# One planned order for all engines: a list scheduler inside a fused attention and maxout kernel

## The chip, the cores and the metric

The kernel runs on one NeuronCore of one Trainium2 chip. The metric is device time in microseconds (us) of that core. A run is one execution; a profiled run also leaves a trace, whose span (first to last instruction) is about 2 us shorter than the run's time. Runs are called slow here when they are over 1.5% above the fastest run of the same kernel.

Engine names: PE is TensorE, DVE is VectorE, ACT is ScalarE, POOL is GpSimd, SP is the engine that issues DMAs here.

## The reference, cut to what matters

```python
def _attn_ref(q, k, v, is_retrieval, n_sink, window):    # q, k, v: (4, 8, 768, 64)
    scores = scale * np.matmul(q, k.transpose(0, 1, 3, 2))
    ...   # retrieval heads: causal; the others: causal and (in a window of 64 or one of 4 sinks)
    scores = np.where(mask[None, :, :, :], scores, -1000000000.0)
    a = np.exp(scores - np.max(scores, axis=-1, keepdims=True))
    a = a / (np.sum(a, axis=-1, keepdims=True) + 1e-09)
    return np.matmul(a, v)

def reference(...):
    x = attn_out.transpose(0, 2, 1, 3).reshape(B * S, H * D)    # 3072 x 512
    return np.maximum(x @ w1, x @ w2) @ w_out                   # d_ff = 1024
```

## The kernel before

The maxout is rewritten as max(x·w1, x·w2) = relu(x·(w1−w2)) + x·w2, so the dense part needs `wd` = w1−w2, and the merged matrix `wm` = w2·w_out, which the kernel builds itself. Attention goes by pairs of heads, 16 pairs in all, four to a batch. A pair needs: loads of q, k, v; casts to bf16 on POOL; PE transposes of q and k, copied out of PSUM; scores in six steps (`S`), exponentials on ACT, masks on DVE; value products (`A`); a normalisation on DVE; a transpose of x (`X`). The dense work of batch b (up matmuls `U`, ReLU, down matmuls `D`) fills PE in the pairs of batch b+1; that of the last batch stands alone at the end.

Only PE is held to the order of the program. The other queues are ordered by the framework's own scheduler. PE's order is written by hand, and a quota decides how much dense work goes into each gap:

```python
    def prep_wd():
        for c in range(KC):
            nc.vector.tensor_sub(out=wd_bf[:, c, :], in0=wts["w1"][:, c, :], in1=w2_bf[:, c, :])
    ...
        # transpose_pair: q's copy always on DVE, k's always on ACT, both strided
        o = t.rearrange("q (m p r) -> q m r p", p=128, r=2)
        i = psb[:, 0:S].rearrange("q (m r p) -> q m r p", p=128, r=2)
        if which == 0:
            nc.vector.tensor_copy(out=o, in_=i)
        else:
            nc.scalar.copy(out=o, in_=i)
    ...
                nc.vector.tensor_relu(out=gts[g][:, f, :], in_=ps[:, 0:GT])     # ReLU always on DVE
    ...
                    nc.scalar.copy(out=ot, in_=ps)                              # output always on ACT
    ...
    with tc.manual_schedule(engines={mybir.EngineType.PE}):
        ...
        for i, cur in enumerate(pairs):
            ...
            if i == 3:
                prep_wo()
                prep_wd()
                fill += [(FC * 512, lambda c=c: w_merge(c)) for c in range(KC)]
            left = 12 - 3 * (i % HP) if b > 0 else 3
            quota = sum(c for c, _ in fill) / left / 3
            first = prev is not None and hp == 0      # first pair of a batch
            qk(*cur, 0)
            if not first:
                spend(quota)
            if prev:
                av(*prev, 4)
                ...
                av(*prev, 5)
            ...
            if first:
                xtr(*prev)
            qk(*cur, 1)
            spend(quota)
            ...
```

The softmax here doesn't subtract the row's maximum and nothing guards it: scores larger than these inputs give would overflow.

## Time and profile before

| | before |
|---|---|
| time, median of 2 runs | 247.19 us (246.89 to 247.49) |
| span of the profiled run, mean granted PE clock | 244.7 us, 0.963 |
| PE, DVE, ACT, POOL busy | 83%, 58%, 52%, 22% |
| first biased exponential of the fifth pair (end of the batch-0 stage) | 61.5 us |
| last x transpose (end of attention) | 213.0 us |

The biased exponential of a pair (`far0` in the code) occurs once per head and marks how far the pair has come. It follows the pair's first scores by 1.4 to 2.1 us, and it is the marker.

From the page of the kernel before: engine, busy us, share of the span, instructions; then busy tenths, PE's granted clock in tenths and the DMA rate in 40 equal slices of 6.1 us.

```profile
...
PE 203.1 (83%) x1888; PEld 114.9 (47%) x1888; DVE 141.0 (58%) x307; ACT 127.2 (52%) x233; POOL 53.8 (22%) x76
...
PE   0587878268599898995998999959989999799994
...
ACT  2387666205626584666657755763747548301001
...
PEclk9999999959689999999999999997999999999999
...
GB/s 142 276 386 227 312 407 291 321 309 234 181 12 11 228 202 145 67 215 161 80 64 110 43 110 0 85 46 0 4 32 57 43 3 43 88 0 43 86 46 86
...
```

PE looks busy from the twelfth slice on, but not before: in the eighth slice (43 to 49 us) it is busy for 20 to 29%. The granted clock drops in slices after that one. PE's busy time also hides waits: the Trainium skill ("Perfetto Trace Analysis", section on per-engine timelines) says that the end of a matmul is estimated by the profiler and not observed. This trace agrees in that eight value matmuls at 108.37 us show 0.41 us, while the next group starts 0.24 us after they did. So the text prices PE's work by starts.

The chain of waits of the kernel before, 38 to 62 us (start, us, what): what the end of batch 0 hung on.

```profile
...
42.66 0.31 DVE wd_bf L157
42.97 0.97 issue
43.95 1.84 DVE wd_bf L157
45.78 0.47 DVE x L284
...
46.74 3.52 DVE wd_bf L157 x2
50.26 0.48 DVE x L284
...
52.27 3.41 PE wmp L169 x8
...
```

DVE did the four wd subtractions between a reciprocal and the multiplication that belongs to it, and between masks. PE had to wait for that normalisation to free its bank, and the next scores stand behind it in PE's fixed order. On ACT the timeline shows one wait of 11.6 us (last bracket: idle before, and who ended it):

```profile
...
56.15 0.87 ACT L231 ACTIVATE at<-sc 128x384 bf16<-128x384 f32 x2 [11.60 <-PE sc L222]
...
```

The timeline at a batch boundary (first pair of the third batch):

```profile
...
111.42 0.61 PE L222 MATMUL sc<-qt,kt 64*128 64x256 bf16 x6
...
111.96 0.48 PE L245 MATMUL po<-vb,at 128*128 128x65 bf16 x10
...
112.58 1.09 DVE L235 TENSOR_TENSOR at<-at,msk 128x512 bf16<-128x512 bf16 x1 [2.87 <-ACT at L231]
...
114.68 0.56 DVE L284 TENSOR_TENSOR x<-po,rez 128x384 bf16<-128x384 f32 x1
...
115.29 0.51 PE L293 MATMUL xtp<-ident,x 128*128 128x128 bf16 x6 [2.85 <-DVE x L284]
...
```

PE ends the value products at about 112.4 us and has nothing queued until the last normalisation on DVE (`x`, from 114.68) is done: 2.85 us idle. DVE is late because it took masks first, and masks wait for ACT.

### The profile page before, as it was taken

Reading aid. Unit: us, or ns where it says so; the run is one execution under the profiler, and the core shown is the slowest. Engines: PE = TensorE matmul, PEld = TensorE weight load, DVE = VectorE, ACT = ScalarE, POOL = GpSimd, SP = SyncE. Lnnn points to the kernel's source line nnn. Section 1 sums busy time; section 2 is a strip of 40 time slices with the busy share of each in tenths; the row PEclk is TensorE's granted clock in tenths of the full one; section 3 lists DMA queues with packets and bytes.
Section 4 is the critical chain, followed back from the end, with each engine's and each line's share of the span. In section 5 each row is a group of like instructions: output and inputs, shape, how many; then the busy total and the mean of one; then the engine's idle time right before and its main releaser. Section 6 shows DMA issues by size and latency. Waiting matters only on the chain.

```text
span 244.7 us, 4799 instructions
## 1 busy us (share of the span) xinstructions
PE 203.1 (83%) x1888; PEld 114.9 (47%) x1888; DVE 141.0 (58%) x307; ACT 127.2 (52%) x233; POOL 53.8 (22%) x76
## 2 busy tenths in 40 slices
PE   0587878268599898995998999959989999799994
PEld 0254654134364545552545555525545555454541
DVE  6966595964666448454864384646653854570510
ACT  2387666205626584666657755763747548301001
POOL 0738381910312121212121211221110100000000
PEclk9999999959689999999999999997999999999999
DMA  5998999998600865285224140210001101201212
GB/s 142 276 386 227 312 407 291 321 309 234 181 12 11 228 202 145 67 215 161 80 64 110 43 110 0 85 46 0 4 32 57 43 3 43 88 0 43 86 46 86
DMA packets 55686, 31.77 MB, mean 130 GB/s; under 512 B 25968, under 2 KB 50544, under 8 KB 55664
## 3 DMA queue, kind: packets, MB, share of 16 engines
q1 hardware_dynamic: 55520, 31.46, 42.9%
q8 instruction: 15, 0.25, 0.4%
q14 instruction: 7, 0.06, 0.1%
q10 hardware_dynamic: 144, 0.01, 0.0%
HBM read 25.17 MB, written 6.29 MB: 129 GB/s over the span
## 4 chain that ended last, share of the span: by engine, by line
PE 62%; DVE 17%; ACT 12%; issue 3%; DMA 2%; POOL 2%; SPq 0%; ACTq 0%; POOLq 0%
PE y L324 26%; PE h L307 12%; PE sc L222 10%; ACT at L231 7%; DVE at L235 6%; PE po L245 5%; PE tp L194 4%; ACT kt L201 3%; PE wmp L169 3%; DVE gt L310 3%; DVE x L284 2%; DMA kn<-in_k_dram 2%; DVE wd_bf L157 2%; PE xtp L293 2%; ACT ot L327 2%
## 5 line engine op out<-in xcount | busy, mean ns | idle before, releaser
L231 ACT ACTIVATE at<-sc 128x512 bf16<-128x512 f32 (+1 forms) x96 | 48.8, 561 | 57.5 <-PE sc L222 57.5
L235 DVE TENSOR_TENSOR at<-at,msk 128x512 bf16<-128x512 bf16 (+1 forms) x96 | 42.7, 451 | 50.5 <-ACT at L231 48.9
L307 PE MATMUL h<-xt,wd_bf 128*128 128x384 bf16 x256 | 51.8, 335 | 2.5 <-DVE gt L310 1.7
L324 PE MATMUL y<-wo_bf,gt 128*128 128x512 bf16 x192 | 48.4, 380 | 0.0
L310 DVE TENSOR_SCALAR gt<-h 128x384 bf16<-128x384 f32 x64 | 35.0, 554 | 19.2 <-PE h L307 18.2
L245 PEld LDWEIGHTS <-at 128*128 128x128 bf16 x672 | 34.3, 104 | 21.8 <-DVE x L284 7.2
L245 PE MATMUL po<-vb,at 128*128 128x65 bf16 x672 | 39.3, 203 | 6.2 <-DVE x L284 6.2
L222 PE MATMUL sc<-qt,kt 64*128 64x256 bf16 (+3 forms) x320 | 32.4, 309 | 5.0 <-ACT kt L201 4.4
L231 ACT ACTIVATE at<-sc,bias_j 128x512 bf16<-128x512 f32 (+1 forms) x64 | 34.0, 593 | 0.0
L307 PEld LDWEIGHTS <-wd_bf 128*128 128x128 bf16 x256 | 23.4, 99 | 21.0 <-issue 10.1
L327 ACT COPY ot<-y 128x512 f32<-128x512 f32 x24 | 14.1, 589 | 35.0 <-PE y L324 34.8
L324 PE MATMUL y<-wm_bf,xt 128*128 128x512 bf16 x96 | 24.6, 379 | 3.5 <-ACT ot L327 2.6
L201 ACT COPY kt<-tp 128x768 bf16<-128x768 bf16 x16 | 16.3, 1020 | 20.8 <-PE tp L194 20.8
L185 POOL CAST vb<-vn 128x768 bf16<-128x768 f32 x16 | 14.7, 918 | 46.4 <-PE po L245 31.0
L182 POOL CAST kb<-kn 128x768 bf16<-128x768 f32 x16 | 15.6, 977 | 41.0 <-PE tp L194 40.3
L324 PEld LDWEIGHTS <-gt 128*128 128x128 bf16 x192 | 16.4, 98 | 17.2 <-issue 3.0
L222 PEld LDWEIGHTS <-kt 64*128 64x128 bf16 x320 | 13.0, 100 | 22.7 <-issue 10.6
L182 POOL CAST qb<-qn 128x768 bf16<-128x768 f32 x16 | 13.9, 870 | 35.2 <-issue 27.0
L231 ACT ACTIVATE at<-sc,bias_94 128x512 bf16<-128x512 f32 x32 | 20.3, 697 | 0.0
L199 DVE COPY qt<-tp 128x768 bf16<-128x768 bf16 x16 | 16.3, 1018 | 3.6 <-PE tp L194 3.2
L194 PE MATMUL tp<-ident,qb 128*128 128x128 bf16 x96 | 9.8, 250 | 8.9 <-DVE bias_94 L128 7.2
L284 DVE TENSOR_TENSOR x<-po,rez 128x384 bf16<-128x384 f32 x32 | 16.8, 552 | 0.1
(41 smaller groups left out, 116.2 us busy)
## 6 DMA issues: line engine op xcount, KB each, us to landing
qn<-in_q_dram SPq DMA_DIRECT2D x16, 384.0 KB, 5.3
kn<-in_k_dram SPq DMA_DIRECT2D x16, 384.0 KB, 4.5
vn<-in_v_dram SPq DMA_DIRECT2D x16, 384.0 KB, 4.8
out_dram<-ot SPq DMA_DIRECT2D x24, 256.0 KB, 2.0
w_151<-in_moe_w_dram SPq DMA_DIRECT2D x2, 1024.0 KB, 9.3
wo<-in_moe_w_out_dram SPq DMA_DIRECT2D x2, 1024.0 KB, 7.6
w_169<-in_moe_w_dram SPq DMA_DIRECT2D x2, 1024.0 KB, 10.9
ir_raw<-in_is_retrieval_dram ACTq DMA_DIRECT2D x1, 8.0 KB, 4.4
```

The lines of the kernel that those rows point to most:

```text
L182: nc.gpsimd.tensor_copy(out=t.rearrange("p n h d -> p h n d"), in_=src.rearrange("p h m (r d) -> p h (m r) d", d=D))
L194: nc.tensor.transpose(psb[:, n * 128:(n + 1) * 128], src[:, n].rearrange("p h d -> p (h d)"), ident)
L201: nc.scalar.copy(out=o, in_=i)
L222: nc.tensor.matmul(sc[hh][:, off:off + w], lhsT=kt[64 * hh:64 * hh + 64, j * 128:(j + 1) * 128], rhs=qt[64 * hh:64 * hh + 64, q0:q0 + w], ...
L231: nc.scalar.activation(out=at[:, 0:n], in_=sc[hh][:, 0:n], func=ACT.Exp, scale=scale, bias=bias)
L235: nc.vector.tensor_mul(out=at[:, 0:n], in0=at[:, 0:n], in1=mk)
L245: nc.tensor.matmul(po[hh][:, i * (D + 1):(i + 1) * (D + 1)], lhsT=at[:, off + t * 128:off + (t + 1) * 128], rhs=vb[:, hh, j, :], start=(st ...
L284: nc.vector.tensor_tensor(out=xs[b][:, :, h * D:(h + 1) * D], in0=po[:, :, 0:D], in1=rez.unsqueeze(2).to_broadcast([128, NB, D]), op=ALU.mult)
L307: nc.tensor.matmul(ps[:, 0:GT], lhsT=wd_bf[:, c, f * 128:(f + 1) * 128], rhs=xts[b][:, c, g * GT:(g + 1) * GT], start=(c == 0), stop=(c == ...
L310: nc.vector.tensor_relu(out=gts[g][:, f, :], in_=ps[:, 0:GT])
L324: nc.tensor.matmul(ps, lhsT=lhsT, rhs=rhs, start=(i == 0), stop=(i == KC + FC - 1))
L327: nc.scalar.copy(out=ot, in_=ps)
```

## The change

The intent is to let one plan decide everything. The kernel describes each piece of work as an `Op` with its possible engines and costs, the ops that it depends on, the buffers that it takes and gives back, and a priority. A list scheduler runs inside the kernel at build time: of all ops that could start, it issues the one that could start earliest, ties going to the better priority. With this the queues of PE, DVE, ACT, POOL and the DMA queue all get a fixed order, the framework reorders nothing, and buffers are fixed tiles handed out by the plan. Five further things come with it: evacuations may go to DVE or ACT (and the casts of the first pair and of the weights to POOL, DVE or ACT); q and k of batches 1 to 3 are loaded in 256-byte runs, so that the copies after the transposes are plain; three value buffers, whose ones are written once; three load buffers (four before); the last dense work uses the four score banks.

The diff, cut to its core:

```diff
+class Planner:
+    def run(self, start):
+        ...
+        while waiting:
+            best = None
+            for op in waiting:
+                for eng, cost in op.engs.items():
+                    r = self.ready_at(op, eng)          # dependencies plus a latency, free buffers
+                    if r is None:
+                        continue
+                    s = max(r, clock[eng])
+                    key = (s if s > now + 1e-9 else now, op.prio, s + cost)
+                    if best is None or key < best[0]:
+                        best = (key, op, eng, s, cost)
+            ...
+            if eng == "PE" and op.row != mode:          # half-row scores or full matmuls
+                mode = op.row
+                cost += SWITCH                          # 0.1
+            ...
+            op.fn(eng)                                  # emits the instructions
 ...
+        "sc": banks[0:4], "po": banks[4:6], "mm": banks[6:8],
+        "ldq": ring("qn", 3, ...), ... "vb": ring("vb", 3, ...), ... "at": ring("at", 12, ...), ...
 ...
+        wide = which < 2 and i < HP
+        pat = ("h (m p r) d -> p h m (r d)", dict(p=128, r=2)) if wide else ("h (n p) d -> p h n d", dict(p=128))
 ...
+            tops.append(P.add({"DVE": 0.56, "ACT": 0.72} if i >= HP else {"DVE": 1.02, "ACT": 1.02}, evac, deps=[t], ...))
 ...
+        batches = [[0, 1], [2, 3], [4, 5]] if i >= HP else [[s] for s in range(NS)]
+            op = P.add({"PE": cost}, go, deps=tops, row=True, prio=(0, i, bt[0]), rel=rel, ...)
+                    e = P.add({"ACT": ...}, exp(st, hh, kind, n), deps=[op, bias_op], ..., prio=(0, i, st, hh))
+                        e = P.add({"DVE": 0.06 + n / 1700.0}, mask(st, hh, n, segs), ..., prio=(1, i, st, hh))
+            norms.append(P.add({"DVE": 0.62}, fn, deps=[last], ..., prio=(0, i, hh)))
 ...
+            wd_ops.append(P.add({"DVE": 1.15}, fn, deps=[ld_ops["w1", c // 2], w2_ops[c]], prio=(3, 2, c)))
+            t = P.add({"PE": FC * 0.2165}, mm, deps=t_ops + wo_ops, ..., prio=(3, 1, c))          # merge
 ...
+        mm = "mm" if b < B - 1 else "sc"
+                ups.append(P.add({"DVE": 0.5, "ACT": 0.5}, relu, deps=[t], ..., prio=(0, 0, f)))
+                e = P.add({"ACT": 0.6, "DVE": 0.6}, evac, deps=[last], ..., prio=(0, 0, 9))       # output
 ...
-    with tc.manual_schedule(engines={mybir.EngineType.PE}):
+    with tc.manual_schedule():
```

## The prediction

> **What bounds it now.** The page gives PE 203 us busy of 244.7 (83%), DVE 58%, ACT 52%; the chain of waits is 62% PE. Busy time flatters PE, so I price its work from unstalled stretches of the timeline: 36 down matmuls in 7.8 us (216 ns each; the Trainium skill, "TensorE: Matmul & The Clock Gate", section on the back-to-back issue gap, states 215.7 ns warm, and this trace agrees), 4 up matmuls in 0.65 us, 8 value matmuls in about 0.25, 6 transposes in 0.33, score pairs of two heads in half their columns. Sum, an estimate: dense 102, merge 8.5, attention 54, together 165 us. Some 80 us are start-up, waits, slow clock and switching.
>
> By stage (timeline, windows):
> - 0 to 60 us, batch 0: pairs' first scores start at 10.2, 18.5, 28.4, 39.2, the fifth pair at 60.1. The fourth takes 21 us: DVE puts four wd subtractions (6.8 us) ahead of masks and normalisations, merge matmuls stand ahead of scores in PE's fixed order, ACT waits 11.6 us in one piece. The granted clock is 0.70 in 50 to 60.
> - 60 to 213, twelve pairs: 12.7 us each, where PE needs about 9.8 (dense 6.4, attention 3.4). At each batch boundary PE waits 3 us for the normalisation; others are short waits on evacuations.
> - 213 to 245: dense work of the last batch, 27.5 us of matmul, nearly full.
>
> **What changes.** No matmul is added or removed; the order listing has the same PE count. (1) One plan orders all engines and puts scores, exponentials and norms before weight preparation. (2) Evacuations go to either DVE or ACT: per two pairs ACT gets 24 exponentials, one key copy, two ReLUs, three output copies; DVE gets six ReLUs. With start-to-start times (exponentials 6.1 us a pair) that is about 16 and 14 us against 20 of PE: neither binds. (3) Later q and k loads use 256-byte runs, so the strided 1.02 us evacuation becomes plain, like the 0.555 us xt copy: 0.4 us on each of 24, mostly off the path except kt before scores. Value loads of that form already land in 4.8 us against 5.3, and DMA share after 112 us is below 0.3. (4) POOL loses 16 memsets; a third value buffer removes its waits on PE. (5) The last dense uses four PSUM banks: about 1 us.
>
> **On the critical path.** Batch 0 is limited by DVE: about 39 us of work after constants end at 7 us, so the fifth pair should start near 48, not 60: -12. The middle: boundary waits (9 us) and half of the evacuation and clock losses: 12.7 to about 11.2 us a pair, -18. Tail: -1 to -2. Score batches need four score banks at once, and two banks still serve up, down and transposes, so I don't expect the full 9.8.
>
> **Predicted: 214 us, 204 to 225 (8 in 10).** Faster by over 2%: 0.95; within 2%: 0.04; slower: 0.01.
>
> **What the profile would show.** Right: fifth pair's scores near 48; ACT's 11.6 us wait gone; no 3 us PE wait for x at pairs 8 and 12; ACT and DVE busy nearly equal; later qt/kt copies near 0.56 (DVE), 0.7 (ACT); pairs 11 to 11.5 us apart; last 31 us hardly changed. Wrong: pairs still 12.5 apart with PE waiting on ReLUs or banks; POOL or PE waiting on q/k loads.
>
> **What would make it wrong.** Durations longer than planned (masks 0.42 to 0.45 where the plan has 0.36), so that fixed orders on five queues block each other; output stores stuck behind loads in the single DMA queue; lower granted clock from denser PE work. Better: PE full, pairs near 10.3, about 203.

## The result, and the profile after

All ratios in this document are the mean time of one kernel's fast runs over that of the other kernel's fast runs of the same rounds, so they are not quite the ratios of the medians quoted. "To the fifth pair" is the time of that pair's first biased exponential, "to the last x transpose" the rest of attention.

| | before | after |
|---|---|---|
| time, median of 2 runs | 247.19 us | 215.53 us (214.73 to 216.34) |
| ratio, 95% interval | | 0.872 (0.857 to 0.887) |
| span, granted clock | 244.7 us, 0.963 | 214.5 us, 0.992 |
| to the fifth pair | 61.5 us | 50.0 us |
| from there to the last x transpose | 151.5 us | 134.1 us |
| last dense work | 31.7 us | 30.4 us |
| PE, DVE, ACT busy | 203.1, 141.0, 127.2 us | 190.4, 128.9, 128.4 us |

The three stages account for the whole difference of the spans: 11.5 + 17.4 + 1.3 = 30.2 us.

The same page lines, of the kernel after:

```profile
...
PE 190.4 (89%) x1872; PEld 108.0 (50%) x1888; DVE 128.9 (60%) x297; ACT 128.4 (60%) x247; POOL 47.6 (22%) x59
...
PE   0388786999999999999999989998999999699993
...
ACT  2489698639873778468845686578458664102021
...
PEclk9999999699999999999999999999999999999999
...
GB/s 115 259 343 318 240 344 409 238 221 219 220 201 248 194 240 222 236 250 209 223 49 55 120 0 3 98 52 0 0 52 98 3 47 52 52 0 98 49 52 98
...
```

The nearly empty slice is gone, and one slice lies well below full clock, not three. DMA now runs at about 220 GB/s in a long even stretch. Before, it came in faster bursts and trickled on: the last load landed at 143.8 us, against 120.1 us after. The experiments come back to it.

The chain of waits of the kernel after, 34 to 56 us:

```profile
...
40.07 2.19 PE bank_80 L461 x6
42.26 0.21 PE bank_75 L331
...
42.82 1.73 PE bank_79 L461 x8
...
44.85 1.74 PE bank_80 L461 x8
46.62 0.70 DVE wm_bf L465
47.36 0.51 PE bank_80 L308 x6
...
48.51 0.28 PE bank_73 L331
...
```

In this run it goes along PE, through the merge matmuls, and not along the wd subtractions. That is not so in every run of this kernel. Here PE had half clock from 38.1 to 41.5 us. The profiled run of e0, the same kernel, had none there; its fifth pair came 1.0 us earlier, and its chain goes over the subtractions and the norms behind them:

```profile
...
39.10 2.35 DVE wd_bf L445 x2
...
41.91 2.35 DVE wd_bf L445 x2
...
45.65 0.68 DVE wm_bf L465
...
```

Of the chain between 10 and 48.5 us, DVE holds 21.4 us in this run and 30.9 us in e0's. So DVE and PE nearly tie at the end of batch 0, and which of them shows depends on the run. PE's longest wait between 30 and 48.5 us is 1.3 us, against 4.2 us before.

The plan put the subtractions in two blocks of two, with masks between, after the third pair's norms and before the fourth's; POOL rested for most of that time. The timelines of the two kernels show the subtractions and POOL's casts beside them. First before, then after:

```profile
...
42.58 3.20 DVE L157 TENSOR_TENSOR wd_bf<-w_169,w_bf 128x1024 bf16<-128x1024 f32 x2
42.89 1.82 POOL L182 CAST kb<-kn 128x768 bf16<-128x768 f32 x1
...
46.66 3.60 DVE L157 TENSOR_TENSOR wd_bf<-w_169,w_bf 128x1024 bf16<-128x1024 f32 x2
47.38 1.81 POOL L182 CAST kb<-kn 128x768 bf16<-128x768 f32 x1
...
```

```profile
...
37.74 2.36 DVE L445 TENSOR_TENSOR wd_bf<-w_f,w_bf 128x1024 bf16<-128x1024 f32 x2
...
40.55 2.36 DVE L445 TENSOR_TENSOR wd_bf<-w_f,w_bf 128x1024 bf16<-128x1024 f32 x2
...
42.03 1.56 POOL L291 CAST qb_90<-qn_82 128x768 bf16<-128x768 f32 x1 [5.70 <-DMA qn_82<-in_q_dram]
...
```

Two subtractions took 3.20 and 3.60 us while POOL cast q, k and v, and 2.36 us each time in the kernel after, the first time with POOL idle. POOL's casts, 0.83 us elsewhere, took 1.8 us beside them. Over all fourteen traces, a subtraction with no cast beside it took 1.20 to 1.22 us, one with a cast beside it 1.21 to 1.84. The Trainium skill ("SBUF — State Buffer", section on who interferes with whom) says that a DVE instruction with two inputs in SBUF contends with a GpSimd instruction that reads SBUF; these lines agree. So the order made the work itself cheaper, by about 2 us, which the prediction did not have.

The timeline of the kernel after at the same batch boundary as above:

```profile
...
115.54 0.22 PE L390 MATMUL bank_78<-vb_94,at_112 128*128 128x65 bf16 x2
...
115.60 1.03 PE L504 MATMUL bank_80<-wm_bf,xt_120 128*128 128x512 bf16 x4
...
116.46 1.89 PE L504 MATMUL bank_80<-wo_bf,gt_122 128*128 128x512 bf16 x8
116.66 0.56 DVE L412 TENSOR_TENSOR x_117<-bank_78,rez_116 128x384 bf16<-128x384 f32 x1
...
118.28 0.28 PE L331 MATMUL bank_73<-qt_97,kt_99 64*128 64x256 bf16 x1
...
118.83 0.51 PE L422 MATMUL bank_79<-ident,x_117 128*128 128x128 bf16 x6
...
```

Between the last value product and the x transpose now stand twelve down matmuls of the batch before (2.7 us) and the next scores. The normalisation on DVE has just that time, and PE does not wait.

### The profile page after: what moved, and what is told of

Read it like the earlier page. It is cut to its first block, busy times and chain, and to the rows that moved or that the text cites. A ratio compares the mean times of both kernels' runs of the same rounds, so it can differ in the third digit from the quotient of the medians.

```text
span 214.5 us, 4691 instructions
## 1 busy us (share of the span) xinstructions
PE 190.4 (89%) x1872; PEld 108.0 (50%) x1888; DVE 128.9 (60%) x297; ACT 128.4 (60%) x247; POOL 47.6 (22%) x59
## 3 DMA queue, kind: packets, MB, share of 16 engines
q1 hardware_dynamic: 73952, 31.46, 60.4%
## 4 chain that ended last, share of the span: by engine, by line
PE 72%; DVE 19%; DMA 3%; ACT 2%; issue 2%; SPq 0%; ACTq 0%; DVEq 0%
PE bank_80 L504 12%; PE bank_79 L504 10%; PE bank_79 L477 6%; PE bank_73 L331 5%; PE bank_77 L390 5%; PE bank_80 L477 5%; PE bank_78 L390 4%; PE bank_75 L331 3%; DMA kn_84<-in_k_dram 3%; PE bank_80 L461 3%; DVE x_117 L412 3%; PE bank_74 L504 2%; PE bank_73 L504 2%; PE bank_79 L422 2%; DVE x_118 L412 2%
## 5 line engine op out<-in xcount | busy, mean ns | idle before, releaser
L504 PEld LDWEIGHTS <-gt_123 128*128 128x128 bf16 x96 | 9.4, 98 | 11.3
L504 PEld LDWEIGHTS <-gt_122 128*128 128x128 bf16 x96 | 9.4, 98 | 11.3
L343 ACT ACTIVATE at_101<-bank_73 128x512 bf16<-128x512 f32 x16 | 9.6, 599 | 4.2 <-PE bank_74 L331 4.2
L343 ACT ACTIVATE at_107<-bank_75,bias_j 128x512 bf16<-128x512 f32 x16 | 11.2, 703 | 0.3 <-PE bank_76 L331 0.3
L343 ACT ACTIVATE at_108<-bank_76,bias_j 128x512 bf16<-128x512 f32 x16 | 11.4, 710 | 0.0
L504 PE MATMUL bank_80<-wo_bf,gt_122 128*128 128x512 bf16 x48 | 11.3, 379 | 0.0
L343 ACT ACTIVATE at_104<-bank_76,bias_64 128x512 bf16<-128x512 f32 x16 | 11.2, 702 | 0.0
L343 ACT ACTIVATE at_109<-bank_73 128x384 bf16<-128x384 f32 x16 | 8.0, 498 | 5.3 <-PE bank_74 L331 5.3
L343 ACT ACTIVATE at_103<-bank_75,bias_64 128x512 bf16<-128x512 f32 x16 | 11.1, 694 | 0.0
L343 ACT ACTIVATE at_105<-bank_73 128x512 bf16<-128x512 f32 x16 | 9.7, 608 | 2.2 <-PE bank_74 L331 2.2
L331 PE MATMUL bank_73<-qt_97,kt_99 64*128 64x256 bf16 (+1 forms) x48 | 9.5, 277 | 1.3 <-DVE kt_99 L315 1.3
L331 PEld LDWEIGHTS <-kt_99 64*128 64x128 bf16 x160 | 5.9, 95 | 9.2 <-issue 6.2
L354 DVE TENSOR_TENSOR at_109<-at_109,msk 128x384 bf16<-128x384 bf16 x16 | 7.5, 469 | 5.1 <-ACT at_109 L343 5.1
L294 POOL CAST vb_94<-vn_87 128x768 bf16<-128x768 f32 x6 | 5.0, 838 | 21.2 <-DMA vn_87<-in_v_dram 9.7
L343 ACT ACTIVATE at_106<-bank_74 128x512 bf16<-128x512 f32 x16 | 9.7, 608 | 0.0
L331 PEld LDWEIGHTS <-kt_100 64*128 64x128 bf16 x160 | 6.0, 94 | 7.3 <-issue 5.5
L343 ACT ACTIVATE at_102<-bank_74 128x512 bf16<-128x512 f32 x16 | 9.6, 598 | 0.0
L331 PE MATMUL bank_74<-qt_97,kt_99 64*128 64x256 bf16 (+1 forms) x48 | 9.3, 275 | 0.2 <-ACT at_106 L343 0.2
L504 PE MATMUL bank_79<-wo_bf,gt_123 128*128 128x512 bf16 x40 | 9.4, 379 | 0.0
```

The lines of the kernel that those rows point to most:

```text
L294: ev(eng)(out=dst[:, :, :, 0:D], in_=src)
L331: nc.tensor.matmul(P["sc", i, st, hh][:, off:off + w], lhsT=kt[64 * hh:64 * hh + 64, j * 128:(j + 1) * 128], rhs=qt[64 * hh:64 * hh + 64, ...
L343: nc.scalar.activation(out=P["at", i, st, hh][:, 0:n], in_=P["sc", i, st, hh][:, 0:n], func=ACT.Exp, scale=scale, bias=bias)
L354: nc.vector.tensor_mul(out=at[:, 0:n], in0=at[:, 0:n], in1=mk)
L504: nc.tensor.matmul(ps, lhsT=lhsT, rhs=rhs, start=(i == 0), stop=(i == KC + FC - 1))
```

## The experiments

Twelve kernels ran, four to a chip, with runs of the kernel before beside each four. Where ratios are compared, both are against the kernel before. The table gives the result of each; the two last columns come from the profiled execution. Profiles marked * fell in a slow run, so their two last columns are not used for small differences. The last column goes from the fifth pair to the end of the span, because some plans move dense work to the tail. Every planned variant is planned anew, so an edit is measured together with the new order that follows from it.

| kernel | median us | ratio (95%) | to the fifth pair | from there to the end |
|---|---|---|---|---|
| before | 247.19 | 1 | 61.5 | 183.2 |
| planned, again (e0) | 215.60 | 0.877 (0.873 to 0.881) | 49.0 | 165.5 |
| engines fixed (e1) | 221.88 | 0.901 (0.895 to 0.906) | 53.5 | 165.5 |
| wide loads (e2) | 220.87 | 0.894 (0.887 to 0.900) | 51.3 | 168.5 |
| before, wd spread (e4) | 242.42 | 0.984 (0.978 to 0.990) | 56.3 | 182.1 |
| only PE and DMA planned (e5) | 227.87 | 0.918 (0.912 to 0.924) | 53.5* | 174.7* |
| before with all parts but the plan (e6) | 244.20 | 0.993 (0.987 to 0.998) | 60.0 | 182.9 |
| single score steps (e7) | 215.08 | 0.875 (0.871 to 0.879) | 48.1 | 164.7 |
| plan without the other parts (e8) | 224.39 | 0.912 (0.908 to 0.917) | 52.6 | 169.7 |
| before, boundary filled (e9) | 241.97 | 0.982 (0.977 to 0.988) | 60.9 | 179.2 |
| shared banks (e10) | 218.80 | 0.889 (0.883 to 0.895) | 50.0 | 165.6 |
| shared banks, single steps, measured costs (e11) | 211.59 | 0.858 (0.852 to 0.864) | 51.0* | 159.3* |
| plain loads everywhere (e12) | 217.97 | 0.884 (0.878 to 0.890) | 55.8* | 162.5* |

The leading theory was that the order of the queues makes the gain. Its rivals were the better balance between DVE and ACT, the shorter copies after plain loads, and the granted clock.

### e0: the planned kernel again, in five rounds

No edit. Expected:

> The planned kernel unchanged, to narrow its interval (two runs so far, 214.7 and 216.3 us, ratio 0.872 within 0.857 to 0.887): 213 to 217 us, ratio 0.866 to 0.880, the middle again 11.0 to 11.2 us a pair. The spread of its clock readings against its times shows what a half-clock stretch costs it; 212.9 us span at clock 1.000 and 214.5 at 0.992 so far.

Measured: 215.60 us, ratio 0.877, as expected. Its six fast runs were also meant to show what the clock costs: the run at mean clock 0.989 had a span of 212.9 us, one at 1.000 had 214.5; the kernel before, in the eleven runs beside it, gave 246.5 us at 0.964 and 245.9 at 0.942. The time does not follow this mean. But the mean is blind to the start: the clock records begin at 32.1 us in the trace before and at 14.2 us in the trace after. Until then, 128-column transposes start 107 ns apart, and later 56 ns apart, so PE ran at half clock for all that time, and the mean counts it as full.

So the rival that the clock makes part of the gain is not excluded. An estimate from the records: between the fifth pair and the last x transpose the kernel before has half clock for 10.2 us (from 62.9 and from 165.2 us), the kernel after for none. That can cost at most half of it, about 5 us. It may be a result of the order as much as a cause: PE pauses less. The Trainium skill ("TensorE: Matmul & The Clock Gate", part on the HAM clock gate) has PE fall to half clock after an idle window of about 3.4 us; the clock records of these traces do show stretches of 3.4 and 6.8 us at half clock, and one begins at 49.2 us in the kernel before, in a wait of PE of 4.2 us. But shorter waits are followed by half clock too: of 2.6 and 2.9 us in the kernel before (62.9 and 165.2 us), and in the kernel after at 38.1 us, where no wait in the 13 us before was over 1.4 us.

### e6 and e8: the parts without the plan, and the plan without the parts

e6 gives the kernel before all that came with the plan, and leaves the ordering as it was:

```diff
+            if b == 0:   # as before
+            else:
+                nc.sync.dma_start(out=t.rearrange("p h m (r d) -> p h (m r) d", d=D),
+                                  in_=src[b, h0:h0 + 2].rearrange("h (n p) d -> p h n d", p=128))
-        vb = cast.tile([128, 2, NB, D + 1], BF16, tag="vb", name="vb")
+        vb = vbs[(b * HP + hp) % 3]                     # ones written once
-        if which == 0:
+        if which == 0 or hp % 2 == 0:                   # copy plain for b > 0
-                nc.vector.tensor_relu(out=gts[g][:, f, :], in_=ps[:, 0:GT])
+                if f in (2, 5):
+                    nc.scalar.activation(out=gts[g][:, f, :], in_=ps[:, 0:GT], func=ACT.Relu)
+                else:
+                    nc.vector.tensor_relu(out=gts[g][:, f, :], in_=ps[:, 0:GT])
```

> The kernel before with every part of the change except the plan: 256-byte loads and plain copies after batch 0, two ReLUs in eight and half of the later k copies moved between DVE and ACT, three value buffers with the ones written once, three load buffers. PE's program order is that of before, the other queues are ordered by the framework. Order theory (the plan's order makes most of the gain): 236 to 243 us. Parts theory (less and better shared evacuation makes it): 228 us or less.

Measured: 244.20 us, ratio 0.993. The parts alone are worth 1 to 2 us. That is less than even the order theory had expected. The parts theory (228 us or less) is out. The waits of PE show why: little changed in what holds PE up (engine and line, waiting for whom: us in total, times, longest). The kernel before, then e6:

```profile
...
PE xtp L293 <- DVE x L284: 9.6, 4, 2.9
...
PE po L245 <- DVE x L284: 6.2, 2, 4.2
...
```

```profile
...
PE xtp L302 <- DVE x L293: 9.5, 4, 2.8
...
PE po L254 <- DVE x L293: 5.3, 3, 3.1
...
```

e8 is the opposite: the planned kernel with the engines of before, wide loads for all pairs, two value buffers and two banks for the last dense work. Beside the order it keeps the three load buffers and the ones written once.

```diff
-        wide = which < 2 and i < HP
+        wide = which < 2
-        "vb": ring("vb", 3, [128, 2, NB, D + 1], BF16),
+        "vb": ring("vb", 2, [128, 2, NB, D + 1], BF16),
-        mm = "mm" if b < B - 1 else "sc"
+        mm = "mm"
-  {"DVE": 0.5, "ACT": 0.5}   # ReLU, and likewise every evacuation with a choice
+  {"DVE": 0.5}
```

> The planned kernel with every other part of the change taken out: evacuation engines of before, wide loads and strided copies for all pairs, two value buffers, the last dense work on two banks. What is left is the planned order (and three load buffers, which it was planned with). Order theory: the parts alone gave about 2 us, so the order alone should give most of the 30: 222 to 229 us. If order and parts only work together (the plan needs the shorter and movable copies to pay off): 232 us or more.

Measured: 224.39 us, ratio 0.912, inside the order theory's range. The order alone takes 8.8% off, the parts alone 0.7%, both together 12.3%. So there are some 7 us (12.3 − 8.8 − 0.7 = 2.8% of 246 us) that need both: the parts, and the order that the plan makes with them.

### e1 and e2: one part taken out of the planned kernel

e1 fixes the engine of every evacuation as before:

```diff
-            engs = {"POOL": 1.0}; if i == 0 and which < 2: engs = {"POOL": 1.0, "DVE": 0.6, "ACT": 0.8}
+            engs = {"POOL": 1.0}
-  {"DVE": 0.5, "ACT": 0.5}   # ReLU
+  {"DVE": 0.5}
-  {"ACT": 0.6, "DVE": 0.6}   # output
+  {"ACT": 0.6}
 # x copy, w2t, wm: DVE; q copy: DVE; k copy: ACT; weight casts: POOL
```

> The planned kernel, but each evacuation keeps the engine that it had before (q copy, x copy, ReLU, weight copies on DVE; k copy and output copy on ACT; the first casts on POOL); the plan still orders everything. Order theory (order of the queues makes the gain, the choice of engine little): 215 to 219 us, the middle still 11.0 to 11.3 us a pair. Balance theory (sharing ReLUs and copies between DVE and ACT makes the gain): 226 us or more, with DVE busy over 138 us and PE waiting on ReLUs, pairs 12 us or more apart.

Measured: 221.88 us, ratio 0.901 against 0.877 for e0: 2.4%, about 6 us. This lies between the two theories. DVE rose to 137.9 us busy, close to what the balance theory said, but the stretch from the fifth pair to the end is as long as e0's (165.5 us in both), though more dense work lies at the end. The 4.5 us by which the two profiled runs differ lie in batch 0 (53.5 against 49.0 us to the fifth pair); for the other 1 to 2 us of the mean there is no trace. So after batch 0 the choice of engine costs little, and in batch 0 it seems to be worth several microseconds. How much of these is the evacuations is open: e1 also puts the casts of the first pair and of the weights back on POOL, and its trace has 10.2 us of half clock in that stretch, e0's none after 14.5 us.

e2 keeps the loads and strided copies of before for all pairs:

```diff
-        wide = which < 2 and i < HP
+        wide = which < 2
-  {"DVE": 0.56, "ACT": 0.72} if i >= HP else {"DVE": 1.02, "ACT": 1.02}
+  {"DVE": 1.02, "ACT": 1.02}
```

> The planned kernel with the loads of before for all pairs: 512-byte runs and the strided 1.02 us copies of q and k in all 16 pairs, not only the first 4. That puts 24 copies x 0.4 us = about 10 us back on DVE and ACT. Order theory (neither engine binds in the middle): 216 to 219 us, and the share of DMA falls back below the planned kernel's. Layout theory (shorter copies make the gain, as they stand before scores): 223 us or more, about 0.8 us more a pair. DMA theory (256-byte runs cost): 213 or less.

Measured: 220.87 us, ratio 0.894 against 0.877: 1.7%, about 4 us, again between the theories, and more than the order theory's "neither engine binds" allowed. The waits of PE say how the longer copy gets onto the path; down matmuls and transposes wait for copies that still hold one of the two shared banks:

```profile
...
PE bank L422 <- DVE x L412: 4.8, 5, 1.5
PE bank L504 <- DVE qt L315: 3.2, 5, 0.8
...
```

In the planned kernel the corresponding wait of the down matmuls for a q copy is not among its PE waits. The DMA queue's share of its engines' time was 52.2% in e2, against 60.4% in the planned kernel, with the same bytes.

### e5: only PE and the DMA queue held to the plan

```diff
-    with tc.manual_schedule():
+    with tc.manual_schedule(engines={mybir.EngineType.PE}):
```

The traces confirm the edit: PE's 1888 matmuls and the DMA issues of SP come in the same order as in e0, while DVE, ACT and POOL are reordered by the framework, DVE by far the most.

> The planned kernel with only PE and the DMA queue held to the plan; DVE, ACT and POOL are ordered by the framework's own scheduler, as before, with the same engine choice, buffers and loads. If the order on the evacuating engines matters: 222 to 235 us, with PE waits for masks, norms or copies back (over 6 us in the middle). If PE's order with the new priorities is enough: 215 to 218 us.

Measured: 227.87 us (225.22 and 226.77 in the fast runs), ratio 0.918, inside the first range. The order on the other engines is worth 4.1% of the time before, about 10 us: about a third of the gain. PE's new order, with the parts, gives the other two thirds. Its profile (a slow run) has 3.9 us of up matmuls waiting for ReLUs on ACT and 4.1 us waiting for q copies on DVE, kinds of waits that sum to about 1.3 us in the planned kernel.

### e4 and e9: the kernel before with one repair each

e4 emits the wd subtractions one by one with the merge steps:

```diff
-                prep_wd()
-                fill += [(FC * 512, lambda c=c: w_merge(c)) for c in range(KC)]
+                fill += [(FC * 512, lambda c=c: (w_merge(c), prep_wd(c))) for c in range(KC)]
```

> The kernel before with one thing changed: the four wd subtractions are emitted one by one with the four merge steps and not in one block ahead of the fourth pair's masks. If the block on DVE is what made the fourth pair 21 us long, the fifth pair's first biased exponential comes at 50 to 54 us (61.5 before, 50.0 planned), ACT's 11.6 us wait is gone, the half-clock stretch at 50 to 57 us is shorter, and the time is 236 to 240 us. If the fourth pair is long for another reason (merge matmuls ahead of scores in PE's order, late weights), 244 to 247 us.

Measured: 242.42 us, ratio 0.984 (0.978 to 0.990), between the two ranges. The fifth pair comes at 56.3 us, later than the 50 to 54 expected, and ACT's longest wait for scores there falls from 11.6 to 4.2 us:

```profile
...
ACT at L231 <- PE sc L222: 5.6, 4, 4.2
...
```

So the block on DVE was a real cause and costs about 4 us, but it is under half of the 11.5 us of batch 0. The rest of that stage is not explained by it; the merge matmuls that stand ahead of scores in PE's order were left where they were.

e9 keeps four down steps back for the two later batch boundaries:

```diff
-            if hp == 0 and b > 0:
-                fill += dense_steps(b - 1)
...
             if first:
+                while fill:
+                    fill.pop(0)[1]()
                 xtr(*prev)
+                acc = 0.0
+                fill += dense_steps(b - 1)
+                quota = (sum(c for c, _ in fill) - 4 * 4 * 512) / left / 3
```

> The kernel before with one change in PE's order: four down steps (16 matmuls, 3.5 us) of the last batch are kept back and run at the two later batch boundaries between the last value product and the x transpose, where PE waited about 3 us for the normalisation. If that wait is what the boundary costs: the waits of PE for x at pairs 9 and 13 are gone and the time is 239 to 243 us. If the DVE queue, not PE's order, sets the boundary, the wait moves and the time stays at 244 to 247.

Measured: 241.97 us, ratio 0.982 (0.977 to 0.988), within the range of the first theory. PE's waits of its x transposes for DVE fall from 9.6 to 3.9 us in total (what remains is the first boundary, 2.6 us, and the end, 1.3 us). Filling the two boundaries by hand gives about 4 us of the middle's 17.4. The gains of e4 and e9 are under the 2% from which a verdict says faster, but their intervals lie clear of 1.

### e12: plain loads for the first four pairs too

```diff
-        wide = which < 2 and i < HP
+        wide = False
-  {"DVE": 0.56, "ACT": 0.72} if i >= HP else {"DVE": 1.02, "ACT": 1.02}
+  {"DVE": 0.56, "ACT": 0.72}
```

> The planned kernel with 256-byte loads for the first four pairs too, so their eight copies take about 0.56 to 0.8 us and not 1.02 (3 us less on DVE and ACT in batch 0). If batch 0 is limited by DVE, as predicted: the fifth pair's first biased exponential at 46 to 48 us (49 to 50 planned) and 212 to 214 us. If batch 0 is limited by what the DMA queue delivers (its share is 1.1 in 10 to 50 us): fifth pair at 51 us or later, 216 to 221 us.

Measured: 217.97 us, ratio 0.884 (0.878 to 0.890) against 0.877 (0.873 to 0.881) for e0. The work on DVE and ACT in batch 0 got shorter, and the kernel did not get faster; the 212 to 214 us of the DVE theory are excluded, and the time lies in the range that was named for the DMA queue. The profile, of a slow run, shows POOL's casts waiting for their loads (waits in 8 to 52 us):

```profile
...
POOL kb L291 <- DMA kn<-in_k_dram: 11.0, 6, 6.5
POOL qb L291 <- DMA qn<-in_q_dram: 7.8, 3, 5.9
...
POOL vb L294 <- DMA vn<-in_v_dram: 5.1, 5, 1.7
...
```

That the queue is the limit does not follow. These waits sum to 23.9 us, but the same waits are 22.2 and 18.1 us in the two traces of the planned kernel, and the chain of waits of e12 from 34 to 58 us goes over the merge matmuls (35%), with half clock from 37.9 to 44.8 us, and over no load. Nor does e12 clear DVE: the same edit that took work from DVE made the loads of q and k dearer. The planned kernel's own traces point to DVE first, busy for 34.4 and 36.1 of the 40 us from 10 to 50, with PE close behind (33.3 and 33.5); POOL waited 5.70 us for the fifth pair's q (the line at 42.03 above), but no load stands in the chain there. What limits e12 stays open.

On the loads themselves, the Trainium skill ("DMA: Bandwidth & Descriptors", specifications) puts the smallest transfer for line rate at 512 bytes. The traces agree: the planned kernel moved 206 GB/s from 60 to 112 us with the DMA engines' share at 1.02 (windows view; it can exceed 1), while 256-byte loads filled the queue. In the same stretch of e2, with q and k in 512-byte runs, it was 186 GB/s at a share of 0.73, which makes about 255 GB/s for a full share (an estimate from these two numbers).

### e7, e10 and e11: what is left in the middle

e7 issues scores in single steps that need two banks, not four:

```diff
-        batches = [[0, 1], [2, 3], [4, 5]] if i >= HP else [[s] for s in range(NS)]
+        batches = [[s] for s in range(NS)]
```

> The planned kernel with the scores of later pairs issued step by step (six groups a pair, two banks each) instead of in three groups that need all four score banks. Switching theory (what is left between the middle's 11.07 and the about 9.8 us of a pair is mostly PE's change between half-row score matmuls and the others, about 0.1 us each way): 216 to 224 us, PE's waits no fewer. Bank theory (what is left is waiting for four free score banks): 205 to 211 us, pairs 10.3 to 10.7 us apart.

Measured: 215.08 us, ratio 0.875: the same as e0, and outside both ranges. The traces show that two effects cancel. At each change from a full matmul to half-row scores PE loses about 0.10 us, and about 0.09 us on the way back. An example is in the timeline after, above: eight down matmuls from 116.46 us, at 0.216 us each, end at 118.19, and the scores start at 118.28; their 1024 columns for two heads at once, at 0.216 us for 512, end at 118.71, and the transposes start at 118.83. From 50 us on, all 70 changes in the planned kernel's trace lose this much, whatever the width of the matmul before; after a 128-column matmul, for example, the next starts 0.151 us later and not 0.056. The planned kernel makes 112 changes, e7 makes 158, so e7 pays about 4.4 us more for them (an estimate, 46 times 0.095 us) and gains about as much elsewhere. The Trainium skill ("TensorEngine Tiling (Array Packing)", key properties) says that changing the tiling mode drains the engine; a loss at each change, in both directions, agrees with that.

e10 puts score banks and matmul banks into one pool of six:

```diff
-        "sc": banks[0:4], "po": banks[4:6], "mm": banks[6:8],
+        "po": banks[4:6], "mm": banks[0:4] + banks[6:8],      # and "sc" -> "mm" in the ops
```

> The planned kernel with the four score banks and the two other matmul banks in one pool of six that scores, transposes, up and down matmuls draw from. If two banks for up, down and transposes hold PE up in the middle (waits that the modelled ends of matmuls hide): pairs 10.7 us apart or less, 210 to 213 us. If banks don't bind there: 214 to 217 us.

Measured: 218.80 us, ratio 0.889 (0.883 to 0.895): slower than e0 by about 1.2% of the time before. Neither expectation holds. More freedom for a greedy scheduler gave a worse order here.

e11 combines both edits and sets three costs of the timing model to what the traces show:

```diff
+  both edits above
-  {"DVE": 0.06 + n / 1700.0}      # mask: 0.36 us for 512
+  {"DVE": 0.06 + n / 1420.0}      # 0.42
-  {"DVE": 1.15}                   # wd subtraction
+  {"DVE": 1.3}
-  {"DVE": 0.5, "ACT": 0.5}        # ReLU
+  {"DVE": 0.55, "ACT": 0.5}
```

> Shared pool of six banks, scores step by step, and three costs of the timing model set to what the traces show (mask 0.42 us, wd subtraction 1.3, ReLU on DVE 0.55). The order puts attention earlier and leaves a longer run of pure dense work at the end, where PE is nearly full. If banks and the grouping by four banks are what is left: 203 to 208 us. If PE's changes of mode eat it: 212 us or more. A version that beats both kernels is looked for here.

Measured: 211.59 us, ratio 0.858 (0.852 to 0.864), fast runs of 210.25, 210.90 and 212.28 us. This beats both kernels: e0's interval (0.873 to 0.881) lies wholly above it. It lies between the two ranges named. Which of its three edits does it is open: each of the first two alone gave nothing or a loss, and the costs were not tried alone. What its order does is visible: attention is pulled ahead (last x transpose at 157.9 us, against 184.4 in e0), and dense work of the last two batches stands as one unbroken block at the end, where PE is nearly full. That alone is not the cause: e7 pulls attention ahead as far (158.8 us) and is no faster than e0.

## Why the prediction was right

The prediction of 214 us (204 to 225) stands against 215.53 and, in more runs, 215.60 us.

1. **Batch 0, −12 us.** Measured: −11.5 us; the fifth pair's first scores come at 48.5 us, predicted 48. ACT's 11.6 us wait is gone. The size was right, and the reason is supported but not isolated. "Batch 0 is limited by DVE" fits e0's trace, where DVE holds 30.9 of the 38.5 us of chain from 10 to 48.5 us; in the first trace it holds 21.4, and the end of the stage goes along PE's merge matmuls. e12, which was to test it, changed the loads as well and does not decide. Of the 11.5 us, spreading the wd subtractions gives about 4 us in time (e4, 5.2 in the marker), and the order alone gives 8.9 in the marker (e8).
2. **The middle, 12.7 to 11.2 us a pair, −18 us.** Measured from the fifth pair's marker to the last x transpose: 151.5 to 134.1 us, −17.4, or 11.2 us for each of twelve pairs. The boundary waits, counted at 9 us, are 9.6 us in the trace before (2.6 at the first boundary, 2.85 at each of the two later ones, 1.3 at the end of attention) and 1.5 us after. All waits of PE in this stretch fall from 16.7 to 4.5 us; with the half clock that went (at most about 5 us, the estimate under e0) that is about the 17.4. By parts: filling the two later boundaries by hand is worth about 4 us (e9), the order of DVE, ACT and POOL about 10 us over the whole kernel (e5), the shorter copies about 4 us, also over the whole (e2). These overlap and do not add up.
3. **Neither DVE nor ACT binds in the middle.** There, from 50 to 184 us after, DVE is busy for 58%, ACT for 68% and PE for 96%, and fixing the engines leaves the time from the fifth pair to the end unchanged (e1). In batch 0 the free choice seems to be worth several us, which the prediction did not list.
4. **Shorter copies "mostly off the path except kt before scores".** Under-sized: without them the kernel is about 4 us slower (e2). The way onto the path is the pair of shared PSUM banks, which a copy holds, more than kt.
5. **Dearer DMAs, taken as nearly free.** After batch 0 no loss shows: e2, with the longer runs, is slower. In batch 0 it is open. The queue is full there (share 1.10 from 10 to 50 us), and POOL waited for q, which the prediction had named as a sign of being wrong, but no load stands in the chain. Landing of q and k went from 5.3 and 4.5 to about 6 us.
6. **Tail, −1 to −2 us.** Measured −1.3 us from the last x transpose on.
7. **What would be wrong about the plan.** Masks do take more than planned and the fixed queues still fit each other: without the wait at the end of attention, PE's waits in 48 to 184 us sum to about 3 us, against about 15 us in 60 to 213 us before.

The main claim is shown from both sides: the order alone makes 8.8% of the 12.3% (e8), the other parts alone 0.7% (e6), and some 7 us need both. Not shown apart is what the clock adds once PE pauses less.

## What to carry to other kernels

When an engine is busy at 83% and still waits, price its work by starts, find the two or three places where another engine's queue holds it up, and repair the order there before making anything shorter: here shorter and movable copies alone gave 0.7%, the same copies under a planned order gave several times that. A scheduler that knows all engines, the buffers and measured durations is worth writing when the order of one queue decides another's; but it is greedy, so try its variants on the chip, since more freedom (shared banks) lost 1.2% alone and a combination won 1.9%. Count the changes between half-row scores and full matmuls, at about 0.1 us each here. Keep weight preparation at low priority, and two-input work on DVE away from POOL's casts (1.84 against 1.22 us for a subtraction here).

## What the Trainium skill lacked or had wrong

- "DMA: Bandwidth & Descriptors" gives 512 bytes as the smallest transfer for line rate, and an overhead for shorter descriptors, but no measured rate of loads below 512 bytes on this chip. These runs show about 206 GB/s at a share of 1.02 while q, k and v come in 256-byte runs, and 186 GB/s at a share of 0.73 with q and k in 512-byte runs (e2).
- "TensorE: Matmul & The Clock Gate" does not say that a profile's clock records can begin only where the first half-clock stretch ends. In the kernel before they begin at 32.1 us, though transposes start 107 ns apart until then, so a mean over the records counts 32 us as full clock.
- "SBUF — State Buffer" says who contends with whom, without a time for a subtraction of an fp32 and a bf16 input beside a cast. Here 128x1024 took 1.2 us with POOL idle and up to 1.84 beside POOL casts, and a cast of 0.83 us took 1.8.
- "TensorEngine Tiling (Array Packing)" says that changing the tiling mode drains the engine, without a time. These traces give it: about 0.10 us at each change into half-row score matmuls and 0.09 us at each change back.
